# Two layers twice over, attention and linear attention, on one core: a planner's gate, one broadcast and its table of settings

## The chip, the cores and the metric

The kernel runs on one core of one Trainium2 chip. The metric is device microseconds of that core, from the first to the last instruction with what lies around them. Before the change, three runs gave a median of 1339.75 us (1339.72 to 1339.89).

## What is computed

Four layers, A B A B, on 2048 tokens of 512 features, with 32 heads of 16:

```
x = x + A(layernorm(x))      # A: multi-query attention, one k and v for all heads
x = x + B(layernorm(x))      # B: linear attention
x = x + A(layernorm(x))
x = x + B(layernorm(x))

A:  p = softmax(q k^T * 16**-0.5);  o = p v;  o @ wo
B:  phi(t) = where(t > 0, t + 1, exp(t)) + 1e-6
    o = phi(q) (phi(k)^T v) / (phi(q) . sum phi(k) + 1e-6);  o @ wo
```

## The kernel before

Tokens are cut into 16 tiles of 128. The same two functions make both pairs of layers: `run_a` (layers 0 and 2) and `run_b` (layers 1 and 3). They do not emit instructions in the order in which they are written. They describe operations, with what each reads and writes, a priority and a guessed duration, and `Planner` plays them through in time and fixes the order of each engine: PE (TensorE), ACT (ScalarE), DVE (VectorE), POOL (GpSimd) and SP (SyncE, the DMA queue). The built program has those orders and waits on semaphores. Any change of a rule or a setting therefore moves instructions everywhere behind it. `TABLE` is a list of pairs (planned time, settings): from that planned time on, those settings hold in place of the defaults in `BASE`.

*Attention.* A block is 128 keys by 512 columns, which are 128 queries of 4 heads. A layer has 16 query tiles x 2 x 16 key tiles x 4 = 2048 of them. PE makes scores in PSUM (L1205, four at a time on strips of 32 rows). Then either ScalarE takes the exponential of two or three neighbouring banks at once (L1402, 128x1024 or 128x1536), or VectorE forms an approximate exponential of one bank by integer arithmetic (L1506). A block of VectorE needs three more copies with a shifted exponent, which GpSimd makes by a 64-bit addition on four blocks at a time (L1548), and so four products with the values on PE instead of one (L1259). ScalarE's banks form two sets of three that take turns. VectorE gets its blocks out of a set (`dve_split`), from a spare bank (`dve_open`) or alone. Whether it may is decided by its backlog in the plan (`BLS`, `BLT`, `SPX`, `BLX`, `DXB`) and by a gate: the key tile `KGATE` of this layer has to be there. When PE has nothing else it runs filler matmuls whose result nobody uses (L1306, and L1190 outside the attention).

Keys are projected in groups of tiles [0] [1] [2, 3] [4 to 7] [8 to 11] [12 to 15] and masked into two tensors (L1071 on ScalarE or L1072 on VectorE). The second attention begins with short segments of its first query tiles, so that scores can start while later tiles are still in layer 1.

*Linear attention.* In layer 1 the denominators come for four tiles at a time: one PE step (L1929), then Ln and Exp with scale -1 on ScalarE (L1933, L1934) give reciprocals of 32 heads on 32 partitions for each tile. `norm1` has to spread each head's reciprocal over its 16 features and multiply it into the queries. It does so in two ways. For tiles 4 to 11 a DMA on SP copies eight rows, each repeated 16 times, into one of three buffers (L1959, buffers in `va` and `rbx`), and VectorE multiplies from there (L1962, both inputs in SBUF). For tiles 0 to 3 and for those in `PEX`, PE multiplies the reciprocals by a matrix of ones, `E4` (L1975 or L1972), and VectorE multiplies out of PSUM (L1980). `main3` then projects the tile (L878) and VectorE adds it to x (L2011). Tiles 4 to 15 of the next layer are transposed by DMA on the same SP queue (L886).

Of the kernel before, what the change touches and what calls it, by code (L numbers as in the profile page):

```python
# [420 lines left out]
class Seg:  # L421
# [55 lines left out]
BLS = 1.6  # L477
SPX = 3.0
BLX = 1.5
BLO = 5.0  # L480
DXB = -1
BLT = 2.5
# [14 lines left out]
DENC = [[0, 1, 2, 3], [4, 5, 6, 7], [8, 9, 10, 11], [12, 13, 14, 15]]  # L497
SW = {1: 0.08, 3: 0.01}
CRIT = 14
KGATE = 7  # L500
RESA = {1: (), 3: ()}
SHIFT = 64.0
ENDL = 14
# [8 lines left out]
FBS = 16  # L512
RES = 4
LOW = 14
AHEAD = 20
# [29 lines left out]
OWNP = 2.0  # L545
HMAX = 0.2
KSP = True
HTOL = 0.02
# [5 lines left out]
DCP = 1.3  # L554
NB1 = 3
VDUR = 0.2
PEX = (12, 13, 14, 15)
DBI = 0.7
FORE = 8
GUARD = 20  # L560
# [1 line left out]
EVP = 1.2  # L562
DPP = 1.5
CHT = 19
# [3 lines left out]
STICK = 1.5  # L568
PBL = 1.2
TABLE = [  # L570
    (5, dict(BLS=1.9, BLX=1.5, HMAX=0.35)),
    (30, dict(BLS=1.9, BLX=2.4, HMAX=0.35)),
    (60, dict(BLS=1.9, BLX=2.4, HMAX=0.2)),
    (270, dict(AHEAD=10, BLX=2.4, HTOL=0.06)),
    (300, dict(AHEAD=10, BLX=2.4, DPP=1.0, HTOL=0.06)),
    (420, dict(AHEAD=10, BLX=2.4, DPP=1.0, DXB=0.3, HMAX=0.1, HTOL=0.06, SPX=2.2)),
    (510, dict(AHEAD=10, BLX=2.4, DPP=1.0, DXB=-1, FBS=12, HMAX=0.1, HTOL=0.06, SPX=2.2)),
    (540, dict(AHEAD=10, BLX=2.4, DPP=1.5, DXB=-1, FBS=12, HMAX=0.1, HTOL=0.06, SPX=2.2)),
    (630, dict(EVP=0.95)),
    (660, dict(EVP=0.95, FBS=22, LOW=20, STICK=0.5)),  # L580
    (720, dict(DXB=0.3, EVP=0.95, FBS=22, LOW=20, STICK=0.5)),
    (780, dict(BLS=1.6, DXB=0.3, EVP=0.95, FBS=22, HTOL=0.06, LOW=20, STICK=0.5)),
    (810, dict(BLS=1.6, BLX=2.4, DPP=1.0, DXB=0.3, EVP=0.95, FBS=22, HTOL=0.06, LOW=20, STICK=0.5)),
    (1050, dict(BLS=1.6, BLX=2.4, DPP=1.0, DXB=0.3, EVP=0.95, FBS=22, HMAX=0.1, HTOL=0.0, LOW=20, STICK=1.0)),
    (1140, dict(BLS=1.6, BLT=2.5, BLX=2.4, DPP=1.0, DXB=0.0, EVP=0.95, FBS=22, HMAX=0.1, HTOL=0.0, LOW=20, STICK=1.0)),
    (1170, dict(AHEAD=32, BLS=1.6, BLT=2.5, BLX=2.4, DPP=1.0, DXB=-1, EVP=0.95, FBS=22, HMAX=0.1, HTOL=0.0, LOW=20, OWNP=1.0, STICK=1.0)),
    (1290, dict(AHEAD=32, BLS=1.6, BLT=2.5, BLX=2.4, CHT=11, DPP=1.0, DXB=-1, EVP=0.95, FBS=22, HMAX=0.1, HTOL=0.0, LOW=20, OWNP=1.0, SPX=1.5, STICK=0.5)),
]
BASE = dict(AHEAD=AHEAD, BLS=BLS, BLT=BLT, BLX=BLX, CHT=CHT, DPP=DPP, DXB=DXB, EVP=EVP, FBS=FBS, HMAX=HMAX, HTOL=HTOL, LOW=LOW, OWNP=OWNP, SPX=SPX, STICK=STICK)


def bass_interleave_layers__grouped_kv_mqa__linear_attn_block__prompt_kernel(
# [11 lines left out]
    pl = Planner(nc)  # L604
    globals().update(BASE)
    for w, c in TABLE:
        pl.at(w, lambda c=c: globals().update({**BASE, **c}))
    op = pl.op
# [587 lines left out]
    def run_a(L):  # L1196
# [250 lines left out]
        def dve_seg():  # L1447
            si = state["si"]
            ahead = 0
            for k in range(si, min(si + 5, len(segs))):  # L1450
                sg = segs[k]
                ahead += len(sg.left)
                least = CHT if si < len(segs) - 1 else ENDL
                if chunk["blk"] and chunk["blk"][-1][0] is sg:
                    least = min(least, CHS)
                if ahead > least and sg.left and all(("K", L, kt) in pl.flags for kt in sg.kts) and ("Q", L, sg.t) in pl.flags:
                    return sg
            return None
# [6 lines left out]
        def dve_want():  # L1465
            sg = dve_seg() if USE_DVE and ("K", L, KGATE) in pl.flags else None
            if sg is None:
                return None
            return min({b[1] for b in sg.left}, key=lambda j: (sg.need[j], -sum(1 for b in sg.left if b[1] == j)))
# [212 lines left out]
    def run_b(L):  # L1682
# [266 lines left out]
        def norm1(t, i, j, rec, b=None):  # L1949
# [132 lines left out]
```

## Time and profile before

| what | value |
|---|---|
| median of three runs | 1339.75 us |
| the profiled execution | 1339.58 us |
| its span, first to last instruction | 1338.1 us |
| PE, DVE, ACT, POOL busy | 1291.6, 1233.7, 1308.2, 1097.9 us |
| granted TensorE clock | 1.0 of full speed in every stretch |
| score blocks on VectorE, of 4096 | 1420 |

The span has six stretches, told apart by the exponentials: a head of 9.5 us, the first attention to 634.8 us (layer 1 starts inside it), the layer change to 658.7, the second attention with layer 1's rest beside it to 690 and without it to 1303.2, and an end of 34.9 us. A line of the timeline gives start, length, engine, line, operation and operands, how many were merged, and in brackets the engine's idle time before it with what ended that.

### The profile page before, as it was taken

How to read it: one execution, taken by the hardware profiler on the slowest of the kernel's cores; microseconds unless marked ns; L12 is line 12 of the kernel's file. 1: busy time of each engine (PE TensorE's matmuls, PEld its weight loads, DVE VectorE, ACT ScalarE, POOL GpSimd, SP SyncE). 2: the span in 40 equal slices, each digit the busy share in tenths (PEclk: the TensorE clock that was granted, in tenths of full speed). 3: DMA queues.
4: the chain of work that ended last, by engine and by line, in shares of the span. 5: the costliest groups of instructions: out<-in, count | busy, mean ns of one | idle time of the engine just before them, and what ended most of it. 6: DMA issues, size and time to landing. Idle time of an engine off the chain costs nothing.

```text
span 1338.1 us, 39100 instructions
## 1 busy us (share of the span) xinstructions
PE 1291.6 (97%) x15353; PEld 430.6 (32%) x15411; DVE 1233.7 (92%) x2227; ACT 1308.2 (98%) x1524; POOL 1097.9 (82%) x1107
## 2 busy tenths in 40 slices
PE   9999999999999999999999999999999999999998
PEld 5222323222232223223732223333233323232235
DVE  8999999999999999997889999999999999999987
ACT  8999999999999999999799999999999999999996
POOL 3799897999989998997017999779899898988980
PEclk9999999999999999999999999999999999999999
DMA  4300000000000000000121000000000000000001
GB/s 112 96 6 13 6 13 6 6 13 2 14 5 14 6 6 6 2 2 2 24 38 21 1 10 10 18 6 6 13 6 9 6 14 6 10 2 1 2 2 64
DMA packets 47076, 20.11 MB, mean 15 GB/s; under 512 B 39728, under 2 KB 46384, under 8 KB 46896
## 3 DMA queue, kind: packets, MB, share of 16 engines
q1 hardware_dynamic: 45840, 17.57, 6.0%
q8 instruction: 125, 2.05, 0.6%
q14 instruction: 55, 0.45, 0.1%
q10 hardware_dynamic: 1056, 0.03, 0.0%
HBM read 5.28 MB, written 2.10 MB: 6 GB/s over the span
## 4 chain that ended last, share of the span: by engine, by line
PE 52%; ACT 30%; issue 8%; DVE 7%; POOL 2%; DMA 1%; SPq 0%; ACTq 0%; POOLq 0%
ACT W L1402 28%; PE ps L1259 22%; PE ps L1205 17%; PE ps L878 4%; DVE W L1506 3%; PE ps L1084 3%; POOL W L1548 2%; PE ps L921 2%; PE ps L1306 1%; ACT phE L1688 1%; DMA va<-va 1%; DVE sacc L1566 1%; PE ps L1814 0%; DMA rbx<-va 0%; DVE st L981 0%
## 5 line engine op out<-in xcount | busy, mean ns | idle before, releaser
L1548 POOL INT64_ADD W<-W x1065 | 1089.2, 1038 | 202.5 <-PE ps L1306 64.8
L1402 ACT ACTIVATE W<-ps 128x1024 bf16<-128x1024 f32 (+1 forms) x1317 | 1245.2, 1131 | 2.4 <-PE ps L1205 2.3
L1506 DVE TENSOR_SCALAR W<-ps 128x512 int16<-128x512 f32 x1420 | 921.6, 682 | 64.9 <-PE ps L1205 50.7
L1259 PE MATMUL ps<-W,VV 128*32 128x512 bf16 x8356 | 635.9, 384 | 4.4 <-DVE sacc L1566 2.8
L1205 PE MATMUL ps<-W,KM 32*128 32x512 bf16 x4096 | 517.3, 385 | 23.2 <-ACT W L1402 13.7
L1205 PEld LDWEIGHTS ps<-W,KM 32*128 32x128 bf16 x4096 | 130.3, 91 | 513.0 <-ACT W L1402 428.4
L1259 PEld LDWEIGHTS ps<-W,VV 128*32 128x32 bf16 x8356 | 151.7, 94 | 257.2 <-issue 170.0
L878 PE MATMUL ps<-wqkv,W 128*128 128x512 bf16 (+1 forms) x226 | 66.0, 368 | 7.7 <-issue 4.3
L1306 PE MATMUL ps<-W,V 128*32 128x512 bf16 (+5 forms) x184 | 52.0, 346 | 0.3 <-DVE W L1506 0.2
L1688 ACT ACTIVATE phE<-ps 128x512 bf16<-128x512 f32 (+1 forms) x66 | 43.8, 665 | 4.5 <-PE ps L1084 3.0
L981 DVE BATCH_NORM_STATS2 st<-x_sb 128x6 f32<-128x512 bf16 x60 | 40.5, 679 | 1.2 <-DMA x_sb<-in_A_x_dram 1.2
L1566 DVE STREAM_TRANSPOSE sacc<-ps 128x512 f32<-128x512 f32 x52 | 36.8, 707 | 3.0 <-PE ps L1259 3.0
L921 PE MATMUL ps<-wo,OT 128*32 128x512 bf16 (+1 forms) x544 | 39.4, 372 | 0.0
L1084 PE MATMUL ps<-W,wqkv 128*128 128x128 bf16 x512 | 38.9, 220 | 0.4 <-DVE W L1695 0.3
L1084 PE MATMUL ps<-W,wq 128*128 128x128 bf16 x464 | 35.1, 221 | 0.4 <-DVE W L1506 0.2
L1084 PEld LDWEIGHTS ps<-W,wqkv 128*128 128x128 bf16 x512 | 29.6, 98 | 11.0 <-issue 8.1
L786 DVE TENSOR_SCALAR phE<-phE 128x513 bf16<-128x513 bf16 x49 | 20.7, 423 | 12.8 <-ACT phE L1688 11.7
L1084 PEld LDWEIGHTS ps<-W,wq 128*128 128x128 bf16 x464 | 26.1, 98 | 12.5 <-issue 8.4
L878 PEld LDWEIGHTS ps<-wqkv,W 128*128 128x128 bf16 x272 | 18.1, 97 | 32.1 <-issue 20.1
L786 DVE TENSOR_SCALAR xn<-x_sb,mv,rs 128x513 bf16<-128x513 bf16 x52 | 26.8, 526 | 0.5 <-ACT rs L972 0.5
L1605 DVE TENSOR_TENSOR Osb<-sacc,ps 128x256 bf16<-128x256 f32 x64 | 26.0, 406 | 0.3
L2011 DVE TENSOR_TENSOR x_sb<-x_sb,ps 128x512 bf16<-128x512 bf16 x30 | 20.4, 682 | 2.5 <-PE ps L878 2.1
(140 smaller groups left out, 483.0 us busy)
## 6 DMA issues: line engine op xcount, KB each, us to landing
out_dram<-x_sb SPq DMA_DIRECT2D x16, 128.0 KB, 1.7
x_sb<-in_A_x_dram SPq DMA_DIRECT2D x6, 256.0 KB, 5.8
wqkv<-in_B_wqkv_dram SPq DMA_DIRECT2D x1, 1536.0 KB, 7.4
va<-va SPq DMA_DIRECT2D x6, 128.0 KB
W<-xn SPq DMA_TRANSPOSE x46, 2.5
x_sb<-in_A_x_dram SPq DMA_DIRECT2D x4, 128.0 KB, 2.2
wq<-in_A_wq_dram SPq DMA_DIRECT2D x1, 512.0 KB, 4.4
wo<-in_A_wo_dram SPq DMA_DIRECT2D x4, 128.0 KB, 3.5
```

The lines of the kernel that those rows point to most:

```text
L786: return e.add_instruction(mybir.InstTensorScalarPtr(name=nc.get_next_instruction_name(), engine=mybir.EngineType.DVE, op0=op0, op1=op1, i ...
L878: return e.matmul(dst, lhsT=l, rhs=r, start=(k == 0), stop=(k == len(pairs) - 1))
L921: ins = e.matmul(ps[32 * q:32 * q + 32, b * 512 + cs.start:b * 512 + cs.stop], lhsT=l[:, q, :], rhs=r, start=start, stop=stop)
L1084: ins = e.matmul(dst[:, g * P:(g + 1) * P], lhsT=lhs(g, k), rhs=rhs(k), start=(k == 0), stop=(k == FT - 1))
L1205: return e.matmul(bank(b), lhsT=KM[r, sg.par, kt * P:(kt + 1) * P], rhs=QT[r, sg.t, :], start=True, stop=True)
L1259: ins = e.matmul(ps[32 * j:32 * j + 32, ACC * 512:(ACC + 1) * 512], lhsT=VV[:, kt, 0 if w is None else 1 + w, :], rhs=ap, start=(k == 0), ...
L1306: o = op({PE: (n / 2400.0, lambda e: e.matmul(ps[32 * j:32 * j + 32, b * 512:b * 512 + n], lhsT=V0[:], rhs=QT[:, sg.t, 0:n], start=st, sto ...
L1402: ex = op({AC: (EXO + 0.4267 * n, lambda e, n=n, s_=s_, p_=p_: e.activation(ws_(p_), ps[:, s_ * 512:(s_ + n) * 512], ACTF.Exp, scale=EXPSC ...
L1506: o = op({DV: (0.602, lambda e: e.tensor_scalar(out=dst.bitcast(I16), in0=bank(b), scalar1=VB, scalar2=VLO, op0=ALU.add, op1=ALU.max))}, w ...
L1548: o = op({PO: (512 * m * PSR + PSO, lambda e, g_=g_, f_=f_: e.int64_add(ws_(g_).bitcast(I64), ws_(f_).bitcast(I64), step))}, reads=wk_(f_) ...
L1566: o = op({DV: (TRD, lambda e, src=src: e.transpose(src, bank(ACC)))}, writes=[B_(ACC)] + key, prio=0.0, lat=0.15)
L1688: op({AC: (0.07 + n / 1200.0, lambda e: e.activation(phE[:, i, 0:n], bank(b, n), ACTF.Exp))}, reads=[B_(b)], writes=[("phE", i)], prio=pr ...
```

## The change

Three edits. `KGATE` goes from 7 to 3, so VectorE may be given score blocks from the fourth key tile on, in both attention layers. `PEX` becomes empty, so tiles 12 to 15 of layer 1 are spread by DMA as tiles 4 to 11 are. `TABLE` is replaced; CHT and HMAX no longer stand in it.

```diff
-KGATE = 7
+KGATE = 3
...
-PEX = (12, 13, 14, 15)
+PEX = ()
...
 TABLE = [
...
-    (780, dict(BLS=1.6, DXB=0.3, EVP=0.95, FBS=22, HTOL=0.06, LOW=20, STICK=0.5)),
...
+    (780, dict(BLS=2.3, EVP=0.95)),
...
+    (870, dict(BLS=2.3, BLT=3.4, BLX=1.5, DPP=1.0, EVP=0.95, HTOL=0.12, STICK=1.0)),
...
 ]
```

The conditions that use them, unchanged:

```
            if not USE_DVE or ("K", L, KGATE) not in pl.flags or (banks.free and not banks.wait and pl.backlog(DV) > SPX) or pl.backlog(DV, 2.0) > BLS or pl.backlog(DV) > BLT:
                return None
...
            if t >= 4 and t not in PEX:
```

In the changed file every line behind the table is two lower: L1402 is L1400 there, L1506 is L1504, L1962 is L1960. The numbers below are each file's own; the texts otherwise use those of before.

How many instructions of a kind the two built programs have:

| | before | changed |
|---|---|---|
| first attention: ScalarE's exponentials of 2 and of 3 banks | 637, 18 | 632, 22 |
| second attention: of 2, of 3 and of 1 | 636, 25, 1 | 647, 18, 1 |
| VectorE's score blocks | 1420 | 1417 |
| products with the values, L1259 | 8356 | 8347 |
| products behind the last scores | 28 | 12 |
| multiplies L1980, L1962 | 8, 8 | 4, 12 |
| GpSimd's shifts | 1065 | 1065 |

The first place is the start of the second attention on PE. Here `W,wq` are query projections, `wkv,W` and `W,wkv` those of values and keys, `W,wqkv` those of layer 1, `W,KM` scores. Before:

```order
L1084 MATMUL ps<-W,wqkv 128x128 x3
L878 MATMUL ps<-W,wkv 128x128 x4
L878 MATMUL ps<-wkv,W 128x16 x4
L1084 MATMUL ps<-W,wqkv 128x128 x13
L1109 MATMUL ps<-W,wq 128x128 x16
L1084 MATMUL ps<-W,wqkv 128x128
L1205 MATMUL ps<-W,KM 128x512 x3
L878 MATMUL ps<-va,W 128x512 x8
L1205 MATMUL ps<-W,KM 128x512 x3
```

And in the changed kernel:

```order
L1082 MATMUL ps<-W,wqkv 128x128 x3
L876 MATMUL ps<-W,wkv 128x128 x4
L876 MATMUL ps<-wkv,W 128x16 x4
L1082 MATMUL ps<-W,wqkv 128x128 x16
L1203 MATMUL ps<-W,KM 128x512 x2
L1082 MATMUL ps<-W,wqkv 128x128 x7
L1107 MATMUL ps<-W,wq 128x128 x16
L1203 MATMUL ps<-W,KM 128x512 x2
L1082 MATMUL ps<-W,wqkv 128x128
L876 MATMUL ps<-va,W 128x512 x5
L1203 MATMUL ps<-W,KM 128x512 x2
```

The first scores moved ahead of the 16 query matmuls of tile 1, and they fill two banks instead of three.

The second place is VectorE at its first score block of the second attention; `x_sb` rows are additions to x, `st`, `mv` and `xn` the layer norm, `VV` the values and `KM` the masked keys. Before:

```order
L1962 TENSOR_TENSOR W<-W,va 128x512
L982 BN_AGGR mv<-st 128x2
L1072 TENSOR_SCALAR KM<-ps,kmask 128x512
L2011 TENSOR_TENSOR x_sb<-x_sb,ps 128x512
L1506 TENSOR_SCALAR W<-ps 128x512
L981 BN_STATS st<-x_sb 128x6
L1570 COPY sacc<-ps 128x512
L1506 TENSOR_SCALAR W<-ps 128x512
L1980 TENSOR_TENSOR W<-W,ps 128x512
```

And in the changed kernel:

```order
L1960 TENSOR_TENSOR W<-W,rbx 128x512
L1070 TENSOR_SCALAR KM<-ps,kmask 128x256
L979 BN_STATS st<-x_sb 128x6
L784 TENSOR_SCALAR xn<-x_sb,mv,rs 128x3x171
L1504 TENSOR_SCALAR W<-ps 128x512
L870 CAST W<-ps 128x512
L980 BN_AGGR mv<-st 128x2
L2009 TENSOR_TENSOR x_sb<-x_sb,ps 128x512
L1504 TENSOR_SCALAR W<-ps 128x512
```

The first score block stood in VectorE's row 652, behind the keys of tiles 4 to 7; now it stands in row 623, right behind those of tiles 2 and 3. Behind the fourth such block, six of the twelve L1962 are still to come.

The third place is the end of the second attention on PE; `W,VV` are products with the values, `wqkv,W` projections of layer 3, `va,sacc` its first sums. Before:

```order
L1205 MATMUL ps<-W,KM 128x512 x3
L1259 MATMUL ps<-W,VV 32x512 x16
L1205 MATMUL ps<-W,KM 128x512
L1259 MATMUL ps<-W,VV 32x512 x20
L878 MATMUL ps<-wqkv,W 128x512 x4
L1259 MATMUL ps<-W,VV 32x512 x8
L1084 MATMUL ps<-W,wqkv 128x128
L1811 MATMUL ps<-va,sacc 128x1 x12
```

And in the changed kernel:

```order
L1203 MATMUL ps<-W,KM 128x512 x3
L1257 MATMUL ps<-W,VV 32x512 x16
L1203 MATMUL ps<-W,KM 128x512
L1257 MATMUL ps<-W,VV 32x512 x8
L1304 MATMUL ps<-W,V 32x512
L1257 MATMUL ps<-W,VV 32x512 x3
L1082 MATMUL ps<-W,wqkv 128x128 x3
L1257 MATMUL ps<-W,VV 32x512
L1082 MATMUL ps<-W,wqkv 128x128
L1809 MATMUL ps<-va,sacc 128x1 x12
```

The four projections went ahead of the last scores, and 12 products instead of 28 are left behind them.

More of the change, by code (lines that the diff above doesn't have):

```diff
@@ L570 @@
 TABLE = [
[L571 to L578, printed above, removed]
@@ L579 @@
-    (630, dict(EVP=0.95)),
-    (660, dict(EVP=0.95, FBS=22, LOW=20, STICK=0.5)),
-    (720, dict(DXB=0.3, EVP=0.95, FBS=22, LOW=20, STICK=0.5)),
-    (780, dict(BLS=1.6, DXB=0.3, EVP=0.95, FBS=22, HTOL=0.06, LOW=20, STICK=0.5)),
-    (810, dict(BLS=1.6, BLX=2.4, DPP=1.0, DXB=0.3, EVP=0.95, FBS=22, HTOL=0.06, LOW=20, STICK=0.5)),
-    (1050, dict(BLS=1.6, BLX=2.4, DPP=1.0, DXB=0.3, EVP=0.95, FBS=22, HMAX=0.1, HTOL=0.0, LOW=20, STICK=1.0)),
-    (1140, dict(BLS=1.6, BLT=2.5, BLX=2.4, DPP=1.0, DXB=0.0, EVP=0.95, FBS=22, HMAX=0.1, HTOL=0.0, LOW=20, STICK=1.0)),
@@ L586 @@
-    (1170, dict(AHEAD=32, BLS=1.6, BLT=2.5, BLX=2.4, DPP=1.0, DXB=-1, EVP=0.95, FBS=22, HMAX=0.1, HTOL=0.0, LOW=20, OWNP=1.0, STICK=1.0)),
-    (1290, dict(AHEAD=32, BLS=1.6, BLT=2.5, BLX=2.4, CHT=11, DPP=1.0, DXB=-1, EVP=0.95, FBS=22, HMAX=0.1, HTOL=0.0, LOW=20, OWNP=1.0, SPX=1.5, STICK=0.5)),
+    (30, dict(AHEAD=10, BLS=1.6, BLT=3.4, FBS=22)),
+    (60, dict(DXB=-1, HTOL=0.06)),
+    (90, dict(DXB=-1, HTOL=0.06, OWNP=4.0, SPX=4.0)),
+    (150, dict(DXB=-1, EVP=2.2, HTOL=0.06, OWNP=4.0, SPX=4.0)),
@@ new lines @@
+    (180, dict(DPP=1.0, DXB=-1, EVP=2.2, HTOL=0.06, LOW=6, OWNP=4.0, SPX=1.5)),
+    (210, dict(DPP=1.0, DXB=-1, EVP=1.2, HTOL=0.06, LOW=6, OWNP=4.0, SPX=4.0)),
+    (270, dict(BLS=1.6, BLT=2.2, DPP=1.5, DXB=-1, EVP=1.2, HTOL=0.06, LOW=6, OWNP=4.0, SPX=4.0, STICK=3.0)),
+    (630, dict(AHEAD=32, BLS=1.6, BLT=2.2, DPP=1.5, DXB=0.0, EVP=1.2, HTOL=0.06, LOW=20, OWNP=1.0, SPX=4.0, STICK=3.0)),
+    (720, dict(EVP=0.95)),
+    (780, dict(BLS=2.3, EVP=0.95)),
+    (810, dict(BLS=2.3, BLX=1.5, DPP=1.0, EVP=0.95, STICK=1.0)),
@@ L588 @@
+    (870, dict(BLS=2.3, BLT=3.4, BLX=1.5, DPP=1.0, EVP=0.95, HTOL=0.12, STICK=1.0)),
+    (900, dict(BLS=2.3, BLT=3.4, BLX=1.5, DPP=1.0, DXB=-1, EVP=1.2, HTOL=0.12, OWNP=2.0, STICK=1.0)),
+    (1110, dict(BLS=2.3, BLT=3.4, BLX=1.5, DPP=1.0, DXB=-1, EVP=1.6, HTOL=0.06, OWNP=2.0, STICK=1.0)),
+    (1290, dict(AHEAD=32, STICK=0.5)),
 ]
-BASE = dict(AHEAD=AHEAD, BLS=BLS, BLT=BLT, BLX=BLX, CHT=CHT, DPP=DPP, DXB=DXB, EVP=EVP, FBS=FBS, HMAX=HMAX, HTOL=HTOL, LOW=LOW, OWNP=OWNP, SPX=SPX, STICK=STICK)
+BASE = dict(AHEAD=AHEAD, BLS=BLS, BLT=BLT, BLX=BLX, DPP=DPP, DXB=DXB, EVP=EVP, FBS=FBS, HTOL=HTOL, LOW=LOW, OWNP=OWNP, SPX=SPX, STICK=STICK)
```

## The prediction

> **What bounds the kernel now.** I start from the busy time by stretch, with the stretches cut at the first and the last exponential of each attention layer. Columns: stretch, its length, then PE, PEld, DVE, ACT and POOL busy with instruction counts, the granted clock, DMA share and GB/s.
>
> ```profile
> 9.50:634.80 625.30, 609.01 (x7254) 187.92 (x7274) 581.52 (x1028) 623.96 (x705) 553.13 (x543) 1.00 0.07 16
> 634.80:658.70 23.90, 23.46 (x364) 19.74 (x367) 21.26 (x56) 16.21 (x41) 0.00 (x0) 1.00 0.14 18
> 658.70:690.00 31.30, 27.77 (x271) 12.11 (x279) 24.99 (x56) 29.05 (x41) 0.00 (x0) 1.00 0.26 39
> 690.00:1303.20 613.20, 593.89 (x7090) 185.54 (x7110) 573.16 (x1003) 612.88 (x696) 537.61 (x525) 1.00 0.04 9
> 1303.20:1338.10 34.90, 30.60 (x309) 19.22 (x309) 26.48 (x60) 21.66 (x33) 0.00 (x0) 1.00 0.18 62
> ```
>
> In the two long stretches ACT (ScalarE) is idle for 1.34 of 625.30 us and 0.32 of 613.20 us. VectorE lacks 44 and 40 us there. PE lacks 16 and 19 us, and part of its busy time is filler (L1306). So 1238.5 of 1338.1 us are the sum of ScalarE's work and nothing else. The waits of ScalarE, next, say the same (us in total, times, longest): its exponentials (L1402) waited 2.3 us in the whole program.
>
> ```profile
> ACT W L1402 <- PE ps L1205: 2.3, 7, 0.7
> ACT W L894 <- PE ps L1109: 0.5, 1, 0.5
> ```
>
> The chain of waits seems to say another thing:
>
> ```profile
> PE 52%; ACT 30%; issue 8%; DVE 7%; POOL 2%; DMA 1%; SPq 0%; ACTq 0%; POOLq 0%
> ```
>
> That is no contradiction. Two sets of banks go back and forth between the engines, and a chain followed backwards steps onto PE whenever a matmul was the last to arrive, even by nothing. The question for a change is which engine has no idle time, and that is ScalarE. ScalarE has slack only between the layers (7.7 us idle of 23.9), in the 31.3 us after that (2.25 us idle) and in the last 34.9 us.
>
> **The price of ScalarE's work.** By shape, an exponential of two banks (128x1024) and one of three (128x1536), first as groups (count, busy, mean ns), then as two runs on ScalarE's timeline (start, length):
>
> ```profile
> L1402 ACT ACTIVATE W<-ps 128x1024 bf16<-128x1024 f32 x1273 | 1189.5, 1119 | 1.3 <-PE ps L1205 1.2
> L1402 ACT ACTIVATE W<-ps 128x1536 bf16<-128x1536 f32 x43 | 63.5, 1500 | 1.1 <-PE ps L1205 1.1
> 1059.22 31.42 ACT L1402 ACTIVATE W<-ps 128x1024 bf16<-128x1024 f32 x34
> 629.13 5.63 ACT L1402 ACTIVATE W<-ps 128x1536 bf16<-128x1536 f32 x4
> ```
>
> The mean of one (1119 ns) overlaps its neighbour; in the run, 34 take 31.42 us, which is 0.924 us each. For three banks the run gives 5.63 / 4 = 1.41 us, with its lead-in included, and the difference of the means gives 0.924 + 0.381 = 1.305 us. I take the middle, 1.36 us.
>
> **The change part by part, against the profiled execution (1339.58 us, span 1338.1; the median of the runs, 1339.75, is 0.17 above it).**
>
> *Score blocks.* The planner was run again, so what counts is how many blocks it now gives to whom. VectorE's falls from 1420 to 1417, with the same 4096 in all. By layer, from the two orders: the first attention layer goes from 637 to 632 two-bank and from 18 to 22 three-bank exponentials, that is -5 x 0.924 + 4 x 1.36 = +0.82 us. The second goes from 636 to 647 and from 25 to 18: +11 x 0.924 - 7 x 1.36 = +0.64 us. Together +1.5 us (with 1.41 and 1.305 for three banks: +1.3 to +1.6). Opening the gate at key tile 3 does start VectorE's blocks sooner, but the new table gives the gain back later: what counts is the total, since ScalarE is busy throughout.
>
> *Copies.* In the second attention ScalarE takes over one copy of 128x512 and loses one of two mask multiplies of 128x256 (L1071) to VectorE:
>
> ```profile
> 1303.73 0.59 ACT L1752 CAST va<-ps 128x512 bf16<-128x512 f32 x1 [0.49 <-PE ps L878]
> 671.80 0.98 ACT L1071 ACTIVATE KM<-ps,kmask 128x256 bf16<-128x256 f32 x2 [0.59 <-PE ps L878]
> ```
>
> That is +0.59 - 0.49 = +0.1 us.
>
> *Start of the second attention.* ScalarE's and PE's timeline there, before:
>
> ```profile
> 657.24 0.60 ACT L1688 ACTIVATE phE<-ps 128x512 bf16<-128x512 f32 x1
> 657.24 1.07 PE L1109 MATMUL ps<-W,wq 128*128 128x128 bf16 x16
> 658.29 0.39 PE L1205 MATMUL ps<-W,KM 32*128 32x512 bf16 x3
> 658.34 0.37 ACT L894 CAST W<-ps 128x256 bf16<-128x256 f32 x1 [0.51 <-PE ps L1109]
> 658.73 1.45 ACT L1402 ACTIVATE W<-ps 128x1536 bf16<-128x1536 f32 x1
> 660.89 1.45 ACT L1402 ACTIVATE W<-ps 128x1536 bf16<-128x1536 f32 x1 [0.70 <-PE ps L1205]
> ```
>
> The 16 query matmuls of tile 1 (1.07 us) stood ahead of the first scores; now they stand behind them, and the first exponential stands ahead of the copy that waited 0.51 us for them. So that wait loses its place, and what is late next is the same copy behind the same matmuls, now with one exponential (0.92 us) beside it. The 0.70 us wait for the second scores can shrink as well. Bounds: nothing, and -1.2 us (both waits gone). I take -0.8 us.
>
> *End.* The last two exponentials, the last products with the values, before, and what waits for them:
>
> ```profile
> 1301.19 2.04 ACT L1402 ACTIVATE W<-ps 128x1536 bf16<-128x1536 f32 x2
> 1302.65 1.04 PE L878 MATMUL ps<-wqkv,W 128*128 128x512 bf16 x4
> 1303.62 0.62 PE L1259 MATMUL ps<-W,VV 128*32 128x512 bf16 x8
> 1304.32 0.72 DVE L1566 STREAM_TRANSPOSE sacc<-ps 128x512 f32<-128x512 f32 x1 [1.74 <-PE ps L1259]
> ```
>
> Four projection matmuls ran between the last scores and the last products; now they run before the last scores, and 12 products follow instead of 28. The last exponential ended at 1303.23 (1301.19 + 2.04), so only what lies behind that can be won: between nothing and the 0.97 us from L878's start to the products'. I take -0.3 us, since the products still have to wait for that exponential.
>
> *Reciprocals of tiles 12 to 15.* Out go four matmuls and four multiplies that read PSUM (L1980); in come four DMAs on SP and four multiplies that read SBUF (L1962). Durations (min/median/max) and the idle time ahead of the second:
>
> ```profile
> L1980 DVE TENSOR_TENSOR W<-W,ps x8: 651/676/689, 648.0 to 716.9; 128x512 bf16<-128x512 bf16 x8
> L1962 DVE TENSOR_TENSOR W<-W,va x6: 408/422/426, 658.4 to 688.0; 128x512 bf16<-128x512 bf16 x6
>   DMA rbx<-va: 1.9, 1
> 664.31 0.61 SPq L1959 DMA_DIRECT2D rbx<-va  x1
> ```
>
> VectorE saves 4 x 0.25 = 1.0 us, and SP issues 4 x 0.6 us more ahead of its transposes. ScalarE's stream hides both: these tiles' keys form the last key group, needed when the early segments run out of the other twelve. I set it at 0. Without the cover, one late landing costs VectorE the 1.9 us above.
>
> Sum: +1.5 + 0.1 - 0.8 - 0.3 = +0.5 us, so 1340.1 for an execution like the profiled one, and 1340.3 with the 0.17.
>
> **The rivals.**
>
> *A, faster: the 31.3 us behind the layer change close up.* VectorE's first score block of the second attention moves some 30 rows up its order, and ScalarE's first exponentials are two banks wide instead of three. If that removes all 2.25 us of ScalarE's idle time there, the time is 1338.0; with the full -1.2 and -0.97 on top, 1337.0. Against it: narrower exponentials ask PE for scores more often, amid projection runs of 1 us.
>
> *B, slower: scores wait for VectorE's banks.* From 780 to 1290 us, the table lets VectorE's backlog reach 2.3 us instead of 1.6 before it is given a block out of a set. The wait that would grow:
>
> ```profile
> PEld ps L1205 <- DVE W L1506: 45.7, 116, 0.5
> L1506 DVE TENSOR_SCALAR W<-ps x1420: 647/681/694, 26.4 to 1297.5; 128x512 int16<-128x512 f32 x178
> ```
>
> Today it costs nothing: while one set waits, the other's exponential runs 0.92 us, and from the scores' start to their exponential are 0.44 us (658.29 to 658.73 above), so ScalarE feels a wait only above 0.48 us. The longest is 0.5. One more score block in VectorE's queue (0.68 us) makes it 1.2 and costs ScalarE 0.7 us; with 7 such, 4.9 us: 1345.2. Against it: the table before allowed 1.9 up to 270 us, and the long stretch that holds it shows 1.34 us of idle time in all.
>
> *C, slower: VectorE and GpSimd in each other's way.* GpSimd's shifts around the layer change, and their mean:
>
> ```profile
> 626.71 3.31 POOL L1548 INT64_ADD W<-W  x3 [0.37 <-DVE W L1506]
> 694.83 3.31 POOL L1548 INT64_ADD W<-W  x3 [64.81 <-PE ps L1306]
> L1548 POOL INT64_ADD W<-W x1065 | 1089.2, 1038 | 202.5 <-PE ps L1306 64.8 <-DVE W L1506 62.8 <-ACT W L1402 20.8
> ```
>
> The eight L1962 ran from 658.4 to 688.0, with GpSimd idle, so no row shows one beside a shift. In the changed order six of twelve stand behind VectorE's fourth score block, when shifts can run. If each waited for one shift, VectorE would lose 6 x 1.04 = 6.2 us, against 6.3 us of idle time in 658.7 to 690 (31.30 - 24.99). I put 0 into the sum by that cover. If the delays hit the score blocks instead, ScalarE may lose about 0.42 us (one multiply's length) at each of six: 1342.8. Beside this stands a rule of the Trainium skill, page "SBUF — State Buffer", section "Who interferes with whom": a VectorE instruction with two inputs in SBUF contends with a GpSimd instruction that reads SBUF, and the second to start blocks fully. By it the old form, with one input in PSUM, was free of this and the new one is not; it speaks against this part of the change, and only the new trace can show it.
>
> **How the numbers follow.** Forecast 1340.3 us, chance 0.62 (own range 1338.6 to 1342.2: the terms' bounds and about a microsecond of waits). A 0.16, B 0.16, C 0.06. A measurement of this kernel can tell 0.2%, 2.7 us, from no change, so faster means below 1337.1 and slower above 1342.4. Below lies only A with every bound in its favour, 0.07. Above lie B and half of C with a little of the forecast's own edge, 0.20. That leaves 0.73. The range runs from 1337.4, most of A, to 1344.2, C and the milder half of B.
>
> **What would show it.** Right: 1279 two-bank and 40 three-bank exponentials at unchanged pitch, ScalarE's idle time below 2.5 us in both long stretches, the first attention longer by 0.8 us and the second by 0.7, an earlier first exponential after the layer change, and fewer microseconds between the last exponential and its transpose. A: ScalarE idle near zero in the 31 us after the layer change. B: L1205's wait for L1506 longer than 0.5 us, and exponentials idle for PE by several us after 780. C: L1962 above 0.42 us, or shifts well above 1.04 us near them. The prediction fails if ScalarE's idle time in the long stretches changes by more than 2 us: the sum holds only while ScalarE never waits.

## The result, and the profile after

The changed kernel takes 1346.47 us (median of 6 runs, 1345.98 to 1346.83), the kernel before 1339.76 beside it: ratio 1.0048, 95% interval 1.0035 to 1.0061, so 6.7 us slower. The forecast was 1340.3, the range ended at 1344.2. The profiled execution spans 1345.1 us. The same five stretches as in the prediction, now cut at the changed kernel's exponentials:

```profile
9.28:635.05 625.77, 615.08 (x7301) 189.69 (x7298) 579.61 (x1026) 625.02 (x704) 553.09 (x543) 1.00 0.07 15
635.05:658.05 23.00, 22.80 (x352) 18.98 (x353) 20.33 (x54) 15.78 (x41) 0.00 (x0) 1.00 0.13 16
658.05:690.00 31.95, 29.09 (x259) 12.78 (x258) 24.86 (x55) 25.81 (x41) 3.36 (x3) 0.89 0.25 37
690.00:1310.87 620.87, 606.52 (x7153) 185.86 (x7153) 571.97 (x1005) 618.32 (x702) 534.50 (x522) 1.00 0.05 9
1310.87:1345.06 34.19, 30.54 (x309) 19.34 (x308) 26.25 (x60) 21.63 (x32) 0.00 (x0) 1.00 0.18 63
```

ScalarE's idle time is length minus the fourth busy time. First attention: 0.75 us (before 1.34). The 31.95 us behind the layer change: 6.14 (before 2.25). The rest of the second attention: 2.55 (before 0.32). So 6.1 us more in the second attention, against a total that grew by 7.0 us from span to span. The new idle time lies ahead of 720 us (behind that it is 0.32 us before and 0.37 after). The row of 657 to 720, which begins inside the layer change, has 5.6 us of it, before and then after:

```profile
657.00:720.00 63.00, 58.05 (x544) 21.92 (x549) 56.09 (x117) 60.19 (x81) 15.45 (x15) 1.00 0.21 35
```

```profile
657.00:720.00 63.00, 57.58 (x508) 21.62 (x505) 53.72 (x112) 54.59 (x77) 18.10 (x18) 0.95 0.27 39
```

ScalarE is idle for 2.81 us of it before and 8.41 after, and PE's mean clock is 0.95. Two places make this up.

**First place, 661 to 675 us.** VectorE's timeline before, then after. L981 (L979 after) is the statistics of a tile's layer norm, L982 (L980) their aggregate, L1962 (L1960) tile 7's multiply by its reciprocals:

```profile
660.84 0.69 DVE L981 BATCH_NORM_STATS2 st<-x_sb 128x6 f32<-128x512 bf16 x1
661.44 0.67 DVE L2011 TENSOR_TENSOR x_sb<-x_sb,ps 128x512 bf16<-128x512 bf16 x1
662.03 0.17 DVE L982 BATCH_NORM_AGGREGATE mv<-st 128x2 f32<-128x6 f32 x1
662.15 0.69 DVE L981 BATCH_NORM_STATS2 st<-x_sb 128x6 f32<-128x512 bf16 x1
663.33 0.43 DVE L1962 TENSOR_TENSOR W<-W,va 128x512 bf16<-128x512 bf16 x1 [0.49 <-DMA va<-va]
```

```profile
663.50 0.43 DVE L1960 TENSOR_TENSOR W<-W,va 128x512 bf16<-128x512 bf16 x1 [1.73 <-DMA va<-va]
663.84 0.69 DVE L979 BATCH_NORM_STATS2 st<-x_sb 128x6 f32<-128x512 bf16 x1
664.44 0.67 DVE L2009 TENSOR_TENSOR x_sb<-x_sb,ps 128x512 bf16<-128x512 bf16 x1
665.03 0.18 DVE L980 BATCH_NORM_AGGREGATE mv<-st 128x2 f32<-128x6 f32 x1
```

The multiply starts when its DMA has landed, in both kernels about 4.4 us after the issue (658.88 to 663.33 and 659.05 to 663.50). Before, the statistics of two tiles ran in that time. After, they stand behind the multiply, and VectorE, which works in the planned order, waits 1.73 us, although the first of them had its input at 661.77 (the residual sum at 661.08 takes 0.69 us). What waits for the statistics, on ScalarE and then on PE:

```profile
665.24 0.29 ACT L968 ACTIVATE ve<-mv,eps 128x1 f32<-128x1 f32 x1 [1.85 <-DVE mv L980]
674.69 1.45 ACT L1400 ACTIVATE W<-ps 128x1536 bf16<-128x1536 f32 x1 [1.61 <-PE ps L1203]
```

```profile
666.75 0.40 PE L1016 MATMUL ps<-ident,xn 128*128 128x128 bf16 x4 [2.72 <-DVE xn L784]
668.25 1.89 PE L1082 MATMUL ps<-W,wq 128*128 128x128 bf16 x16
```

ScalarE's first wait is 1.85 us; behind it stand the reciprocals of tiles 8 to 11, so tile 8's DMA goes out late and its multiply starts at 670.53 instead of 668.10. (That it waits 1.55 us there is no consequence of the first wait: in x1 below, where that one is gone, it waits 1.52.) PE pauses 2.72 us, and its 16 query matmuls then take 1.89 us instead of the 1.07 of before. The clock's column says why:

```profile
664.00:667.00 3.00, 0.28 (x5) 0.23 (x4) 2.57 (x6) 1.76 (x5) 0.00 (x0) 1.00 0.00 0
667.00:670.00 3.00, 3.00 (x27) 1.93 (x24) 1.76 (x4) 1.91 (x4) 0.00 (x0) 0.60 0.37 47
670.00:674.00 4.00, 4.00 (x17) 1.28 (x15) 1.48 (x3) 2.92 (x3) 0.00 (x0) 0.50 0.26 34
```

**Second place, 690 to 715 us.** The multiplies of tiles 11, 13 and 14 wait 0.86, 0.44 and 0.72 us for their DMAs, and tile 12's is slow. On VectorE, GpSimd and PE:

```profile
694.82 1.00 DVE L1960 TENSOR_TENSOR W<-W,rbx 128x512 bf16<-128x512 bf16 x1
```

```profile
692.88 2.67 POOL L1546 INT64_ADD W<-W  x3 [4.86 <-DVE W L1504]
```

```profile
696.11 1.04 PE L876 MATMUL ps<-va,W 128*128 128x512 bf16 x4 [1.05 <-DVE VV L1049]
```

The multiply took 1.00 us instead of 0.42. The shifts ended at 695.55, the multiply 0.27 us later. The VV product (L1049, a multiply that forms the values) behind it was late, and PE waited 1.05 us for that.

### The profile page after: what moved, and what is told of

The parts are those of the page before. It is cut to its first block, busy times and chain, and to the rows that moved or that the text cites. A ratio compares the mean times of both kernels' runs of the same rounds, so it can differ in the third digit from the quotient of the medians.

```text
span 1345.1 us, 39244 instructions
## 1 busy us (share of the span) xinstructions
PE 1311.1 (97%) x15444; PEld 432.8 (32%) x15444; DVE 1229.4 (91%) x2224; ACT 1311.2 (97%) x1527; POOL 1097.9 (82%) x1107
## 4 chain that ended last, share of the span: by engine, by line
PE 55%; ACT 25%; issue 7%; DVE 5%; POOL 5%; DMA 1%; ACTq 0%; POOLq 0%; SPq 0%; DVEq 0%
ACT W L1400 24%; PE ps L1257 24%; PE ps L1203 18%; POOL W L1546 5%; PE ps L876 5%; PE ps L1082 3%; DVE W L1504 2%; PE ps L919 2%; PE ps L1304 2%; ACT phE L1686 1%; DVE st L979 1%; DMA va<-va 1%; PE ps L1188 1%; DMA rbx<-va 0%; DVE sacc L1564 0%
## 5 line engine op out<-in xcount | busy, mean ns | idle before, releaser
L1400 ACT ACTIVATE W<-ps 128x1024 bf16<-128x1024 f32 (+1 forms) x1320 | 1248.6, 1123 | 5.1 <-PE ps L1203 4.9
L1504 DVE TENSOR_SCALAR W<-ps 128x512 int16<-128x512 f32 x1417 | 920.3, 683 | 71.7 <-PE ps L1203 55.1
L876 PE MATMUL ps<-wqkv,W 128*128 128x512 bf16 (+1 forms) x272 | 76.8, 371 | 0.3 <-DVE sacc L1693 0.2
L1304 PE MATMUL ps<-W,V 128*32 128x512 bf16 (+6 forms) x223 | 60.8, 339 | 0.4 <-DVE W L1693 0.3
L979 DVE BATCH_NORM_STATS2 st<-x_sb 128x6 f32<-128x512 bf16 x60 | 40.7, 681 | 0.9 <-DMA x_sb<-in_A_x_dram 0.7
L1304 PEld LDWEIGHTS ps<-W,V 128*32 128x32 bf16 x223 | 17.4, 95 | 25.6 <-issue 16.7
```

Source lines behind the costliest of these rows:

```text
L876: return e.matmul(dst, lhsT=l, rhs=r, start=(k == 0), stop=(k == len(pairs) - 1))
L979: op({DV: (0.6, lambda e: e.bn_stats(st[:, t, 0, :], x_sb[:, t, :]))}, reads=[("x", t)], writes=[("st", t)], prio=prio, lat=0.13)
L1304: o = op({PE: (n / 2400.0, lambda e: e.matmul(ps[32 * j:32 * j + 32, b * 512:b * 512 + n], lhsT=V0[:], rhs=QT[:, sg.t, 0:n], start=st, sto ...
L1400: ex = op({AC: (EXO + 0.4267 * n, lambda e, n=n, s_=s_, p_=p_: e.activation(ws_(p_), ps[:, s_ * 512:(s_ + n) * 512], ACTF.Exp, scale=EXPSC ...
L1504: o = op({DV: (0.602, lambda e: e.tensor_scalar(out=dst.bitcast(I16), in0=bank(b), scalar1=VB, scalar2=VLO, op0=ALU.add, op1=ALU.max))}, w ...
```

## The experiments

Where an edit moves a multiply, it does so in VectorE's finished order, and nothing else is planned again; `move(a, b)` puts a right behind b, `ahead(a, b)` right ahead of it, `later(a, n)` n instructions back. `mul7` is tile 7's multiply, `stats2_3` the statistics of tile 3 in layer 2. The other edits, x2's fillers apart, run the planner again, so that the split of the score blocks shifts too; the work planned for ScalarE's exponentials is compared by 0.918 us for two banks, 1.336 for three and 0.48 for the single one, their mean pitch in the trace of before.

### One multiply moved, both ways

```diff
 # x1_mul7_later: the changed kernel
+    move("mul7", "stats2_3")
 # x3_mul7_sooner: the kernel before
+    ahead("mul7", "stats2_2")
```

> The changed kernel with one instruction moved: VectorE's multiply of tile 7 of layer 1, which waited 1.73 us for its DMA, stands behind the two layer-norm statistics of tiles 2 and 3 of layer 2, as it did before the change. Theory M (that wait holds back the statistics, PE then sits idle for 2.72 us, the granted clock falls to 0.5 for 6.8 us): no PE gap over 1.5 us there, clock 1.00 throughout, 1341.5 us (1340.3 to 1342.7). Rival D (the DMA spreads of tiles 12 to 15 themselves cost the time): these stay, so 1346.5 within 0.8 and the clock may fall all the same. Rival G (VectorE's early score blocks and the port shared with GpSimd): unchanged, 1346.5 within 0.8.

> The kernel before with the opposite move alone: VectorE's multiply of tile 7 ahead of the statistics of tiles 2 and 3, as the changed kernel has it; gate, spreads and table are those of before. Theory M: VectorE waits near 1.7 us for the DMA, PE idles over 2 us, and if the clock falls 1344.5 us (1343.5 to 1346.5), if it happens to hold 1341.5. Rivals D and G: 1339.8 within 0.8, since none of the three edits is in it.

Measured: x1 1343.68 us (ratio 1.0027, 1.0016 to 1.0037), 2.8 us less than the changed kernel. x3 1342.65 (1.0018, 1.0009 to 1.0028), 3.0 us more than the kernel before. PE's timeline in x3 is like the changed kernel's, with a pause of 3.37 us:

```profile
666.91 0.61 PE L1018 MATMUL ps<-ident,xn 128*128 128x128 bf16 x4 [3.37 <-DVE xn L786]
```

So one waiting multiply ahead of two statistics is worth about 3 us, in either kernel, with no change in any engine's work; part of that is the fallen clock that follows it (next section). x3 came out below the 1343.5 to 1346.5 that I expected with a fallen clock. x1 came out above its expected 1342.7: the first place is mended, the second is not, and there the clock now falls:

```profile
690.76 1.03 DVE L1960 TENSOR_TENSOR W<-W,rbx 128x512 bf16<-128x512 bf16 x1
```

```profile
692.08 1.79 PE L876 MATMUL ps<-va,W 128*128 128x512 bf16 x4 [1.05 <-DVE VV L1049]
```

### Is it the wait or the clock?

In x2_warm, PE's last filler matmul (`f_`) ahead of the 2.72 us pause is issued 42 times, so that PE stays busy and VectorE's order stays as it is.

```diff
 # x2_warm: the changed kernel
+    def many(e, fn=f_.fn):
+        for _ in range(42):
+            ins = fn(e)
+        return ins
+    f_.fn = many
```

> The changed kernel with the last filler ahead of the 2.72 us gap on PE issued 42 times instead of once (about 2.2 us of matmuls on zero weights); no order is changed and VectorE's wait stays. It parts the clock from the wait. Theory M: the clock stays at 1.00, which gives back the half-rate loss of up to 3.4 us, while VectorE's wait and ScalarE's 1.85 us behind it stay: 1343.6 us (1342.8 to 1344.8). If the clock's fall costs nothing: 1346.5 within 0.6. If all the loss is the clock's: 1341.

Measured: 1346.18 us (1.0045, 1.003 to 1.006), a miss. The clock is 1.00 in every row, and ScalarE's wait stayed:

```profile
666.03 0.29 ACT L968 ACTIVATE ve<-mv,eps 128x1 f32<-128x1 f32 x1 [1.84 <-DVE mv L980]
```

So the clock is not the main cost. But the 0.3 us between the medians is not its price either. From 657 to 690 us ScalarE is idle for 6.23 us in the changed kernel and for 4.48 in x2, so the clock was worth up to 1.75 us there; from 690 to 720, 0.97 us of that is lost again, where tile 14's multiply waits 1.53 us for its DMA instead of 0.72. The changed kernel, then x2:

```profile
657.00:690.00 33.00, 30.14 (x273) 13.48 (x271) 25.87 (x58) 26.77 (x43) 3.36 (x3) 0.90 0.25 38
690.00:720.00 30.00, 27.45 (x236) 8.14 (x235) 27.85 (x55) 27.82 (x35) 14.74 (x15) 1.00 0.29 40
```

```profile
657.00:690.00 33.00, 31.20 (x332) 15.70 (x334) 27.19 (x62) 28.52 (x45) 3.36 (x3) 1.00 0.30 43
690.00:720.00 30.00, 26.19 (x233) 8.08 (x233) 27.72 (x55) 26.85 (x34) 14.92 (x15) 1.00 0.26 37
```

Executions of one and the same kernel point the same way. The changed kernel took 1345.98 to 1346.27 us in the three with a mean clock of 0.999 and 1346.66 to 1346.83 in the three with 0.997; x3 took 1341.64 to 1341.98 in four with 0.998 or 0.999 and 1342.53 to 1343.07 in six with 0.997. By medians the lower clock goes with 0.6 us in the one and 1.0 in the other.

### The planner told the true landing time

The plan counts a spread as 0.7 us of issue and 1.6 until it has landed. d1_dbl makes the second number fit the 4.4 us of the trace.

```diff
 # d1_dbl: the changed kernel
-DBL = 1.6
+DBL = 3.7
```

> The changed kernel planned anew with the landing of a spread's DMA set to 3.7 us instead of 1.6 (the trace shows 4.4 us from issue to the multiply, 0.7 of them the issue). Everything behind the layer change is ordered anew. Theory M: the planner no longer puts such a multiply ahead of work that is ready; waits of VectorE for these DMAs fall from 5.3 us to under 1.5, no clock fall, 1340 us (1338 to 1342). Rivals D and G: the spreads and early blocks are still there, 1344 to 1347.

Measured: 1342.17 us (1.0018, 1.0009 to 1.0027), 4.3 us less than the changed kernel. That is just above the expected 1338 to 1342 and below the rivals' 1344. The multiplies wait 0.62 us in all, against 5.30. What is left is of the size of the planned work: the new plan gives VectorE 1413 blocks and ScalarE 3.2 us more exponentials than the kernel before.

### Four more multiplies moved

```diff
 # x4_muls_later: the changed kernel
+    move("mul7", "stats2_3")
+    later("mul11", 2)
+    later("mul13", 4)
+    later("mul12", 4)
+    later("mul14", 2)
```

> Changed kernel, with tile 7's multiply behind the statistics of tiles 2 and 3 as in x1, and four more multiplies that wait for a DMA or a port moved back in VectorE's order by 2 to 4 instructions: those of tiles 11, 12, 13 and 14. Waiting-multiply theory: the 3.0 us that ScalarE still loses to waits from 690 to 720 us in x1 fall below 1 us, PE has no pause of 1 us there and no fall of its clock; 1341.1 us (1340.4 to 1342.0). Rival, that VectorE and GpSimd block each other in these multiplies wherever they stand: multiplies of about 1.0 us appear at the new places, ScalarE's waits stay near 3 us and the time at 1343 to 1344.5.

Measured: 1341.31 us (1.0015, 1.0005 to 1.0024), in the expected range: 5.2 of the 6.7 us come back with every engine's work unchanged. The rest is of the size of the 1.5 us of planned exponentials. Tile 8's multiply still waits 1.49 us there; ScalarE is idle for no more than 0.3 us above the kernel before, so a wait alone costs little. The rival shows too, in one multiply that met a shift at its new place; two score blocks came late behind it, and PE and ScalarE (0.65 us at 704.79) waited for those:

```profile
700.94 1.26 DVE L1960 TENSOR_TENSOR W<-W,va 128x512 bf16<-128x512 bf16 x1
```

```profile
704.35 0.39 PE L1203 MATMUL ps<-W,KM 32*128 32x512 bf16 x3 [0.68 <-DVE W L1504]
```

### Each edit alone, or all but one

```diff
 # r3_pex: the kernel before
-PEX = (12, 13, 14, 15)
+PEX = ()
 # r1_pex: the changed kernel
-PEX = ()
+PEX = (12, 13, 14, 15)
 # t1_table: the kernel before with the new TABLE
 # r4_kgate: the kernel before
-KGATE = 7
+KGATE = 3
```

> Kernel before, with its old table and gate, and only the reciprocals of tiles 12 to 15 spread by DMA. ScalarE's planned exponentials are the same as before to 0.2 us, and tile 7's multiply stands behind the statistics as before. Waiting-multiply theory: the edit alone costs little, 1340.3 us (1339.3 to 1341.8). Rival, that the edit costs 2 to 3 us by itself (four more DMA landings that VectorE waits for, or multiplies that meet shifts): 1342 to 1343.5, with the waits in VectorE's rows of these four multiplies.

> Changed kernel, with the reciprocals of tiles 12 to 15 spread by PE again as before; new table and gate stay. VectorE gets 1413 score blocks, so ScalarE's exponentials grow by 1.7 us (2.4 against the kernel before), and tile 7's multiply still stands ahead of the statistics. Waiting-multiply theory: 1339.8 + 2.4 + 0.8 of other work + about 3 for that multiply = 1345.5 us (1344 to 1347), with PE's pause of 2.7 us near 664 still there. Rival, that the DMA spread of tiles 12 to 15 is what costs: all of the 6 us beyond the work goes, 1341 to 1343.

> Kernel before with the new table alone (gate at key tile 7 and the reciprocals by PE as before). VectorE gets 1401 score blocks instead of 1420, and the exponentials planned for ScalarE add up to 8.1 us more. If the sum of ScalarE's planned work sets the time: 1347.9 us (1346.5 to 1350). Tile 7's multiply stands behind the statistics here, so no pause near 664 by the waiting-multiply theory. Rival, that the plan's split matters less than the waits: 1341 to 1344.

> Kernel before with the gate at key tile 3 alone (old table, reciprocals by PE). VectorE gets 1401 score blocks instead of 1420 and the exponentials planned for ScalarE add up to 8.1 us more, so 1347.7 us (1346.5 to 1350) from the work alone; waits for multiplies can only add to it. Rival, that an earlier start of VectorE's blocks helps by itself: below 1345 us.

Measured: r3 1348.51 us (1.007, 1.0054 to 1.0085), r1 1348.18 (1.0062, 1.0047 to 1.0078), t1 1352.52 (1.0097, 1.0081 to 1.0113), r4 1364.11 (1.0178, 1.0164 to 1.0192). All four lie above what I expected, and none is faster than the three edits together (r1's interval overlaps the changed kernel's). The planned work accounts for +0.3, +3.1 (I had counted 2.4), +8.1 and +8.0 us; most of the rest is ScalarE's idle time from 657 to 720 us (table below). r1 speaks against the spread of tiles 12 to 15 as the cause in the changed kernel: without it nothing comes back (it has 1.6 us more planned work than the changed kernel, and takes 1.7 us more). r3 shows that the same edit alone costs 9 us on the old table, by the same kind of wait. Its VectorE and PE:

```profile
688.05 0.43 DVE L1962 TENSOR_TENSOR W<-W,va 128x512 bf16<-128x512 bf16 x1 [1.90 <-DMA va<-va]
688.39 0.32 DVE L1051 TENSOR_TENSOR VV<-ps,wts 128x160 bf16<-128x160 f32 x1
...
690.17 0.42 DVE L1962 TENSOR_TENSOR W<-W,rbx 128x512 bf16<-128x512 bf16 x1 [1.37 <-DMA rbx<-va]
690.51 0.68 DVE L2011 TENSOR_TENSOR x_sb<-x_sb,ps 128x512 bf16<-128x512 bf16 x1
```

```profile
688.76 0.23 PE L878 MATMUL ps<-wkv,W 128*128 128x16 bf16 x3 [2.05 <-DVE VV L1051]
...
691.25 1.89 PE L878 MATMUL ps<-W,wkv 128*128 128x512 bf16 x4 [1.17 <-DVE x_sb L2011]
```

In r4 the waits are longest: 3.13 us of VectorE ahead of one multiply, and PE's pause behind it:

```profile
701.15 0.43 DVE L1962 TENSOR_TENSOR W<-W,va 128x512 bf16<-128x512 bf16 x1 [3.13 <-DMA va<-va]
```

```profile
702.24 0.19 PE L878 MATMUL ps<-wkv,W 128*128 128x16 bf16 x1 [4.55 <-DVE W L1506]
```

### How far the order can mend the spread alone

```diff
 # r5_pex_later: r3_pex
+    later("mul14", 3)
+    later("mul13", 4)
+    later("mul11", 4)
+    later("mul12", 4)
 # r6_pex_later2: the same with 5 for mul14 and 6 for mul11
```

> Kernel before with the reciprocals of tiles 12 to 15 spread by DMA alone (r3_pex, 1348.5 us), and four multiplies moved back by 3 or 4 instructions in VectorE's order: those of tiles 12 and 11, which waited 1.90 and 1.37 us for their DMA ahead of a VV product and a residual sum that PE needed, and those of tiles 13 and 14. Waiting-multiply theory: PE's pauses of 2.05 and 1.17 us near 687 and 690 go, with its half clock, and most of the 9 us comes back: 1341.3 us (1340.3 to 1343). Rival, that the four added DMAs cost by themselves (SyncE's queue, landing of three in a row, shared engines): 1345 us or more, with the pauses moved to other waits.

> As r5_pex_later (1346.1 us), with two of its multiplies moved back by 2 more instructions: tile 11's, which still waited 0.80 us for its DMA ahead of an aggregate of the statistics and a copy of the keys, behind these two; and tile 14's, which took 1.05 us beside a shift on GpSimd ahead of a VV product, behind that product. If such a multiply costs through what stands behind it, whether it waits for a DMA or for GpSimd, PE's pauses of 1.33 and 1.10 us and the two stretches of half clock go: 1342 us (1340.8 to 1343.8). Rival, that the added DMAs cost by themselves: 1345 to 1346.5.

Measured: r5 1346.09 us (1.0044, 1.0031 to 1.0058), r6 1344.73 (1.0034, 1.0021 to 1.0046). Both miss what the waiting-multiply theory expected: r5 lies in its rival's range (1345 or more), r6 0.3 us below its rival's. In r5, tile 14's multiply took 1.05 us beside a shift, and PE waited for the VV product behind it:

```profile
702.27 1.05 DVE L1962 TENSOR_TENSOR W<-W,va 128x512 bf16<-128x512 bf16 x1
...
703.70 0.31 DVE L1051 TENSOR_TENSOR VV<-ps,wts 128x160 bf16<-128x160 f32 x1
```

```profile
704.06 0.36 PE L1306 MATMUL ps<-W,V 128*32 128x448 bf16 x1 [1.10 <-DVE VV L1051]
```

Behind that pause PE's clock fell again: 20 products with the values took 2.33 us there, and 1.26 in r6. In r6 that pause is gone, and the one near 690 is what stays. SyncE issues three spreads in a row, and tile 11's own projection waits for the second of them:

```profile
683.73 0.63 SPq L1959 DMA_DIRECT2D va<-va  x1
684.42 0.61 SPq L1959 DMA_DIRECT2D rbx<-va  x1
685.08 1.94 SPq L1959 DMA_DIRECT2D va<-va  x1
```

```profile
691.21 0.43 DVE L1962 TENSOR_TENSOR W<-W,rbx 128x512 bf16<-128x512 bf16 x1 [0.87 <-DMA rbx<-va]
```

```profile
691.69 1.03 PE L878 MATMUL ps<-va,W 128*128 128x512 bf16 x2 [2.27 <-DVE W L1962]
```

From the second issue to that multiply are 6.8 us, with 0.87 of waiting at the end, against 4.4 for a spread that was alone. With the old table this DMA is therefore late for PE itself, and no later place of the multiply hides it while PE keeps its order. In what share the three in a row and the transposes on the same queue make it late was not tried.

### A version faster than both

The kernel before has two such multiplies of its own (0.49 and 1.91 us of wait).

```diff
 # b1_later: the kernel before
+    later("mul7", 1)
+    later("mul9", 4)
```

> Kernel before with two multiplies of its own that wait for a DMA moved back in VectorE's order: tile 7's (0.49 us of wait) behind one aggregate of the statistics, tile 9's (1.91 us) behind the VV product, residual sum, statistics and aggregate that stand next. Waiting-multiply theory: PE's pauses of 1.32 us near 663.6 and 1.05 us near 670 shrink, and of the 2.8 us that ScalarE loses from 660 to 690 about 1 us goes: 1338.5 us (1337.9 to 1339.3). Rival, that such short waits are covered by other slack: 1339.5 us, no change.

Measured: 1338.09 us, ratio 0.9985 (0.9976 to 0.9994), in the expected range and 1.8 us below the kernel before: faster, by less than the 0.2% that I had called measurable, though the interval leaves out 1. Tile 9's multiply no longer waits, and PE's pause of 1.05 us near 670 is gone:

```profile
670.75 0.39 DVE L1962 TENSOR_TENSOR W<-W,rbx 128x512 bf16<-128x512 bf16 x1
```

### All runs in one table

Idle is ScalarE's from 657 to 720 us, 63.00 less its busy time in rows like the two shown above; work is the planned exponentials against the kernel before; their sum would be the difference in time if nothing else changed. Waits are those of VectorE for the DMAs of multiplies, 655 to 730 us.

| kernel | waits | idle | idle against before, plus work | measured |
|---|---|---|---|---|
| before | 2.40 | 2.81 | | |
| changed | 5.30 | 8.41 | 5.6 + 1.5 = +7.1 | +6.7 |
| x1_mul7_later | 3.11 | 5.31 | 2.5 + 1.5 = +4.0 | +4.1 |
| x2_warm | 6.32 | 7.63 | 4.8 + 1.5 = +6.3 | +6.6 |
| x3_mul7_sooner | 3.03 | 6.30 | 3.5 + 0 = +3.5 | +3.0 |
| d1_dbl | 0.62 | 2.84 | 0.0 + 3.2 = +3.2 | +2.5 |
| x4_muls_later | 1.49 | 3.13 | 0.3 + 1.5 = +1.8 | +1.8 |
| r3_pex | 6.52 | 9.44 | 6.6 + 0.3 = +6.9 | +9.0 |
| r5_pex_later | 3.12 | 7.11 | 4.3 + 0.3 = +4.6 | +6.2 |
| r6_pex_later2 | 3.22 | 7.03 | 4.2 + 0.3 = +4.5 | +5.0 |
| r1_pex | 3.91 | 6.99 | 4.2 + 3.1 = +7.3 | +8.7 |
| t1_table | 4.97 | 5.48 | 2.7 + 8.1 = +10.8 | +13.0 |
| r4_kgate | 11.32 | 18.84 | 16.0 + 8.0 = +24.0 | +24.3 |
| b1_later | 0.70 | 1.88 | -0.9 + 0 = -0.9 | -1.8 |

Work plus idle time of ScalarE in these 63 us gives most of each difference, to 0.9 us in nine of thirteen kernels. In r3, r5, r1 and t1 it falls 1.4 to 2.2 us short. In r3, r5 and r1 1.0 us of that is idle time behind 720 us (1.32, 1.32 and 1.28 us against 0.32 before, in short waits of up to 0.3 us); the rest stays open. Part of the agreement is luck, too: over the whole span of the changed kernel ScalarE is busy for 1311.2 us against 1308.2, 3.0 us more and not 1.5, and its idle time outside these 63 us is 1.5 us less. The two cancel. Why it is busy for more than the count gives was not tested.

## Why the prediction was wrong, point by point

- **ScalarE's stream hides the spread's waits (0 us): the step that failed.** The text asked when the last tiles' keys are needed and found time. It did not ask what stands behind the multiply on VectorE while the DMA is under way: statistics, residual sums and VV products that ScalarE and PE need within a microsecond. x1 and x3 put about 3 us on one such place, x4 5.2 us on five, and r3 9 us on the edit alone. The step looked at tiles 12 to 15 only, while the new plan had placed all twelve multiplies anew. The price that I named without the cover, 1.9 us for a late landing, was VectorE's own wait; in x3, 1.9 us more of wait ahead of that multiply (2.40 against 0.49) cost 3.0 us.
- **The multiply that cost most was not one of the four changed.** Tile 7's, 2.8 us by x1, was spread by DMA before as well; the new plan only put it ahead of the statistics. My count of instructions by kind could not show that; the order around each waiting instruction does.
- **Score blocks (+1.5).** Borne out within about half a microsecond. The counts hold (1279 and 40 exponentials). x4, which has the changed kernel's work and few of its waits, stands at +1.8, with an end that is 0.6 us shorter and 0.3 us more idle time from 657 to 720. The first attention grew by 0.6 us (0.8 forecast), but its idle time fell by 0.5 us, which was not forecast.
- **Start (-0.8).** From the last exponential to the first of the next attention: 23.00 us after 23.97, so -1.0, inside the bounds, but not by the mechanism. The two waits that were to shrink, 0.51 and 0.70 us, are 0.36 and 0.84 us afterwards:

```profile
659.43 0.37 ACT L892 CAST W<-ps 128x256 bf16<-128x256 f32 x1 [0.36 <-PE ps L1107]
661.62 1.02 ACT L1400 ACTIVATE W<-ps 128x1024 bf16<-128x1024 f32 x1 [0.84 <-PE ps L1203]
```

Behind six banks, at the logarithm of the reciprocals, ScalarE stands 27.5 us behind the last exponential before the change and 27.7 after it. Up to there nothing was won; that the number came out is luck.
- **End (-0.3).** Behind the last exponential: 34.19 after 34.81, so -0.6, inside the bounds and by the mechanism: its transpose starts 0.59 us after that exponential's end instead of 1.08.
- **Rival A, the 31 us close up:** the contrary; idle time there went from 2.25 to 6.14 us. The time of 1346.5 lies near rival B's 1345.2, but that is chance, as the next point shows.
- **Rival B, scores waiting for VectorE's banks:** did not happen. The row that was to show it reads, after,

```profile
PEld ps L1203 <- DVE W L1504: 44.9, 123, 0.6
```

That is 44.9 us against 45.7, and the longest 0.6 against 0.5; ScalarE's idle time from 780 to 1290 us went from 0.32 to 0.37 us.
- **Rival C, VectorE and GpSimd in each other's way:** the mechanism is there, at a smaller price. Of the twelve multiplies three touched a shift; I had priced six. Tile 12's began 0.10 us after a shift and took 1.00 us. Tile 10's began 0.02 us ahead of one and kept its 0.41 us; there the shift waited, so that the train of three took 3.55 us instead of the 3.31 of the prediction. At tile 15's it was a shift again that waited. VectorE and GpSimd at tile 10's:

```profile
686.71 0.41 DVE L1960 TENSOR_TENSOR W<-W,va 128x512 bf16<-128x512 bf16 x1
```

```profile
684.46 3.55 POOL L1546 INT64_ADD W<-W  x3 [54.16 <-DVE W L1504]
```

In x1, x2, x4, d1, r3 and r5 again one multiply is slow, at 1.02 to 1.26 us. What it costs hangs on what stands behind it: about 0.65 us of ScalarE in x4; in r5, where a VV product and then a fallen clock did, 1.78 us. The rule of the Trainium skill, page "SBUF — State Buffer", section "Who interferes with whom", that an instruction with two inputs in SBUF blocks against GpSimd's reads and that one with a single such input does not, agrees with these rows: before, the form with one input in PSUM took 0.67 us, its usual time, beside shifts, as VectorE and then GpSimd show:

```profile
706.66 0.67 DVE L1980 TENSOR_TENSOR W<-W,ps 128x512 bf16<-128x512 bf16 x1
```

```profile
702.15 6.11 POOL L1548 INT64_ADD W<-W  x6 [4.02 <-PE ps L1205]
```

- **The sum's condition broke, as the text had said it might.** I wrote that the sum holds only while ScalarE never waits, and that a change of its idle time by over 2 us would break it. It changed by 6.1 us, and in the table work plus idle time follows the runs to 0.9 us in nine of thirteen.

## What to carry to other kernels

An instruction that waits for a DMA on an engine that works in order costs whatever stands behind it, so look there first: list the next few instructions, and who waits for them. Place it by the time from issue to landing that the trace shows (4.4 us here for one alone, where the plan had 2.3), not by when its own result is needed. And when a planner is run again, edits do not add up: these three cost 9, 13 and 24 us alone and 6.7 together, because each plan deals out the score blocks anew and happens to place the waiting instructions elsewhere.

## What the hardware showed that I had not expected

The granted clock fell to half in pieces of 3.41 us: 3.41 in x1, 6.83 in the changed kernel and in x3, 10.24 in r3, by the trace's record of the clock. A single pause of 1.05 us stood ahead of one such fall (x1, above), and one of 1.33 us ahead of another (r5), while the kernel before has pauses of 1.32 and 1.05 us at 664 and 670 and no fall, so the length of one pause does not decide alone. The Trainium skill, page "TensorE: Matmul & The Clock Gate", section "Part 1: The HAM clock gate (the "warmup" mystery)", gives an idle window of about 3.4 us for it; the pieces agree with that length, but the pauses that led to them here were shorter. The fall cost less than the waits. Between executions of one kernel, a mean clock of 0.997 instead of 0.999, which is one piece more (half of 3.41 us is 0.0013 of 1345), goes with 0.6 us in the changed kernel and 1.0 in x3. With the clock held up by filler matmuls (x2) the time went down by only 0.3 us, since a later wait took most of the gain.
